# One written order for three engines from the first instruction on: the first batch's attention, its mixing and the weight conversion at fixed places, and k loaded first

## The chip, the cores and the metric

The kernel runs on one core of one Trainium2 chip. The metric is the device time of one execution in microseconds (us). Before the change it is 1892.02 us, the median of 3 runs (1890.05 to 1893.53). Six names come back throughout: PE is the matrix engine (TensorE), DVE the vector engine, ACT the scalar engine, POOL the GpSimd engine, SP the engine whose queue issues almost all DMAs, and PEld is the loading of a matmul's stationary operand, which overlaps PE.

## What is computed

Eight batches of 576 tokens go through three stages, all in fp32: attention with keys and values averaged over groups of 8 tokens, a mixing layer of rank 32 with a feed-forward block behind it, and a Fourier mixing with normalisation and a second feed-forward block.

```python
# attention: q, k, v are (8 batches, 8 heads, 576, 64)
k_p = k.reshape(B, H, 72, 8, D).mean(axis=3)
v_p = v.reshape(B, H, 72, 8, D).mean(axis=3)
scores = scale * np.matmul(q, k_p.transpose(0, 1, 3, 2))
attn = softmax(scores)
x = np.matmul(attn, v_p)              # laid out as (8, 576, 512)
# first block: U (576, 32), V (32, 576), w_ch1 (512, 2048), w_ch2 (2048, 512)
h = x.transpose(0, 2, 1) @ U @ V
u = x + h.transpose(0, 2, 1)
x = u + np.maximum(u @ w_ch1, 0.0) @ w_ch2
# second block, with weights of its own
u = x + np.real(np.fft.fft(np.fft.fft(x, axis=1), axis=2))
un = (u - mean(u)) / np.sqrt(var(u) + 1e-06)
out = u + np.maximum(un @ w_ch1, 0.0) @ w_ch2
```

## The kernel before

**Number format.** A matmul runs on fp32r operands, so each fp32 number is kept as a high part and a low part (`split`: ACT copies the high part, a subtraction on DVE or POOL gives the low part), and one product is three matmuls: high by high, high by low, low by high. The weights arrive as 64-bit floats. For each tile of 128 x 512 weights ACT runs two operations (`high`, L146 and L149) and DVE two integer operations (`bits`, L153 and L154) that build fp32; then comes `split`, on ACT and POOL. `w_first` does this for the 32 tiles W[k, f] of the first block: k = 0 is the first layer, k = 1 the second, f = 0 to 15 a slice of 128 of the 2048 hidden channels.

**Stages.** The work of the first block is cut into groups. A group takes 512 tokens through the feed-forward block: for each f, `st1` makes 12 matmuls of 512 columns into the hidden slice (tile h; its inputs are the transposed tokens utx, called `xs` in the code), ACT and DVE form the high and low part hh and hl, and `st2` of the slice before makes 12 matmuls of 512 columns that add into four output banks (o, o, h, m). One f is called a slot here. Groups 0 to 5 go this way. From about 800 us on, the rest of the first block and all of the second go through a form with 7 products instead of 8 (tiles x, wr).

**What runs beside the groups.** Between the pieces of a slot, generators ("lanes") are stepped: `lane_a` is the attention of batches 1 to 7, one tile of 128 tokens at a time (`kq`: scores and exponentials; `exp_turn`: transposition; `av`: product with v, normalised into x, split into xh and xl; `hu_mm`: the product with U, two matmuls on xh and xl, made right behind the next tile's `kq`), and from batch 3 on the mixing of the batch before (`mix_one`) beside it. `lane_prep` loads and pools k and v. `w_first`, later `w_combine` and `w_second`, convert and combine weights. `pair_prep` reloads the mixed tokens `ud` of the next group from memory, and turns (`turn`, a DVE transpose) and splits them (`settle`) into utx.

**The first batch.** Nothing of group 0 can start before batch 0 has been through attention (`first`, `tile_steps`), the product with U (tile hu, `hu_mm`), the mixing with V (`mix_split`, `mix_mm`; tiles hst, vst) and the transposition (`block_prep`, L826). Three tiles are in flight at a time, on three pairs of PSUM banks (s, o, h). The weight conversion starts in the same stretch.

**What sets the order.** A scheduler of the framework orders each engine's instructions by its own estimate of times, unless `manual_schedule` is on: then the instructions of the engines named stand in the order of the code. Before the change, this holds for PE, ACT and DVE from group 1 on:

```python
    for gi, js in enumerate(groups):
        if gi == 1:
            order.enter_context(tc.manual_schedule(engines={mybir.EngineType.PE, mybir.EngineType.Activation, mybir.EngineType.DVE}))
```

SP and POOL stay with the scheduler in both kernels. Each engine works off its own list strictly in order, and waits on semaphores of the others.

## Time and profile before

| what | value |
|---|---|
| median of 3 runs | 1892.02 us (1890.05 to 1893.53) |
| profiled execution, its own time | 1891.17 us |
| its span, first to last instruction | 1889.1 us |
| PE busy | 1812.9 us, 96% of the span |
| DVE, ACT, POOL busy | 54%, 37%, 10% |
| mean granted clock of PE | 0.984 of full speed |

How to read it: a busy share is the time with an instruction under way. The profiled execution takes 2.07 us more than its span (1891.17 against 1889.1), and lies 0.85 us under the median of the runs. The granted clock is 1.0 at 2.4 GHz and 0.5 at 1.2 GHz; values between are a mean over a stretch that has both. "Idle before" is the time that an engine stood still ahead of an instruction, and the name behind the arrow is what ended it. Matmuls are pipelined, so the times of neighbours overlap.

### The profile page before, as it was taken

How to read it: one execution, taken by the hardware profiler on the slowest of the kernel's cores; microseconds unless marked ns; L12 is line 12 of the kernel's file. 1: busy time of each engine (PE TensorE's matmuls, PEld its weight loads, DVE VectorE, ACT ScalarE, POOL GpSimd, SP SyncE). 2: the span in 40 equal slices, each digit the busy share in tenths (PEclk: the TensorE clock that was granted, in tenths of full speed). 3: DMA queues.
4: the chain of work that ended last, by engine and by line, in shares of the span. 5: the costliest groups of instructions: out<-in, count | busy, mean ns of one | idle time of the engine just before them, and what ended most of it. 6: DMA issues, size and time to landing. Idle time of an engine off the chain costs nothing.

```text
span 1889.1 us, 29426 instructions
## 1 busy us (share of the span) xinstructions
PE 1812.9 (96%) x10424; PEld 1588.1 (84%) x10424; DVE 1029.2 (54%) x2275; ACT 700.1 (37%) x1992; POOL 191.2 (10%) x341
## 2 busy tenths in 40 slices
PE   5898899999999999999999999999999999999999
PEld 4676788788778888899999889989989999999998
DVE  7783667666756444444455655565554444444332
ACT  6662445545544222233333433333323323232321
POOL 4340132122200000000010000000000000000000
PEclk8898999999999999999999999999999999999999
DMA  9652657867857622567678767777777675757564
GB/s 360 243 162 71 186 176 214 260 218 233 247 169 211 194 87 72 186 226 247 223 232 260 268 206 224 226 235 227 218 225 210 201 236 173 238 180 228 184 208 133
DMA packets 264467, 391.90 MB, mean 207 GB/s; under 512 B 61504, under 2 KB 92320, under 8 KB 264320
## 3 DMA queue, kind: packets, MB, share of 16 engines
q1 hardware_dynamic: 263392, 386.61, 64.7%
q0 software_dynamic: 928, 3.40, 0.6%
q8 instruction: 83, 1.36, 0.3%
q14 instruction: 64, 0.52, 0.1%
HBM read 311.55 MB, written 78.38 MB: 206 GB/s over the span
## 4 chain that ended last, share of the span: by engine, by line
PE 83%; DVE 8%; DMA 3%; ACT 3%; issue 2%; SPq 1%; DVEq 0%; ACTq 0%
PE h L114 39%; PE o L114 19%; PE m L114 10%; PE hu L114 7%; PE s L114 7%; PE s L936 1%; DVE scr L154 1%; DMA ul<-ud 1%; DVE x L107 1%; DVE x L577 1%; ACT xh L110 1%; DVE scr L153 1%; PE s L563 1%; DMA raw<-vr 1%; DVE hl L1024 1%
## 5 line engine op out<-in xcount | busy, mean ns | idle before, releaser
L114 PEld LDWEIGHTS h<-x,wr 128*128 128x128 f32 x4032 | 529.1, 191 | 24.3 <-DVE side L107 0.2
L114 PE MATMUL h<-x,wr 128*128 128x256 f32 x4032 | 548.4, 284 | 0.0
L114 PE MATMUL o<-w,hh 128*128 128x512 f32 x1152 | 328.5, 395 | 3.1 <-ACT hh L1023 3.1
L114 PE MATMUL h<-utx,w 128*128 128x512 f32 (+1 forms) x1164 | 285.3, 394 | 16.4 <-ACT utx L110 11.3
L114 PEld LDWEIGHTS h<-utx,w 128*128 128x128 f32 x1164 | 217.6, 191 | 62.3 <-ACT utx L110 11.7
L114 PEld LDWEIGHTS o<-w,hh 128*128 128x128 f32 x1152 | 202.8, 189 | 34.9 <-ACT hh L1023 4.0
L114 PE MATMUL o<-w,hl 128*128 128x512 f32 x576 | 192.3, 392 | 0.0
L107 DVE TENSOR_TENSOR side<-h,side 128x256 f32<-128x256 f32 x192 | 106.3, 554 | 153.5 <-PE h L114 153.0
L114 PE MATMUL m<-w,hh 128*128 128x512 f32 x576 | 166.1, 396 | 0.0
L1319 ACT ACTIVATE hh<-side 128x256 fp32r<-128x256 f32 x192 | 99.9, 521 | 119.7 <-DVE side L107 112.7
L1024 DVE SCALAR_TENSOR_TENSOR hl<-h,hh 128x512 fp32r<-128x512 f32 x96 | 66.2, 690 | 136.4 <-ACT hh L1023 135.9
L1319 ACT ACTIVATE hh<-h 128x256 fp32r<-128x256 f32 x96 | 36.9, 384 | 272.4 <-PE h L114 270.5
L1325 DVE SCALAR_TENSOR_TENSOR hl<-h,hh 128x256 fp32r<-128x256 f32 x96 | 40.7, 424 | 171.3 <-ACT hh L1319 171.3
L114 PEld LDWEIGHTS o<-w,hl 128*128 128x128 f32 x576 | 108.2, 188 | 24.3
L1325 DVE SCALAR_TENSOR_TENSOR hl<-side,hh 128x256 fp32r<-128x256 f32 x192 | 105.9, 551 | 29.4 <-ACT hh L1319 29.4
L114 PEld LDWEIGHTS m<-w,hh 128*128 128x128 f32 x576 | 103.2, 191 | 17.0
L1023 ACT ACTIVATE hh<-h 128x512 fp32r<-128x512 f32 x96 | 57.4, 598 | 145.7 <-PE h L114 140.7
L555 ACT ACTIVATE s<-s,mx 128x72 f32<-128x72 f32 x280 | 83.0, 331 | 61.8 <-DVE mx L551 61.2
L114 PE MATMUL hu<-w,hh 128*128 128x512 f32 x384 | 104.7, 394 | 0.0
L114 PE MATMUL m<-w,hl 128*128 128x512 f32 x288 | 97.9, 394 | 0.0
L104 POOL TENSOR_TENSOR wo<-wo 128x256 fp32r<-128x256 f32 x88 | 66.3, 772 | 261.8 <-ACT wo L110 124.2
L104 DVE TENSOR_TENSOR x<-ul,x 128x256 fp32r<-128x256 f32 x154 | 59.3, 420 | 46.5 <-ACT x L110 46.5
(254 smaller groups left out, 2414.4 us busy)
## 6 DMA issues: line engine op xcount, KB each, us to landing
wr<-wc SPq DMA_DIRECT2D x336, 512.0 KB
wc<-wo SPq DMA_DIRECT2D x88, 256.0 KB
x<-x SPq DMA_DIRECT2D x48, 256.0 KB
ur<-ud SPq DMA_DIRECT2D x36, 256.0 KB
x1d<-ur SPq DMA_DIRECT2D x36, 256.0 KB
ul<-u2d SPq DMA_DIRECT2D x36, 256.0 KB
ur<-u2d SPq DMA_DIRECT2D x36, 256.0 KB
out<-ur SPq DMA_DIRECT2D x36, 256.0 KB
```

The costliest lines, as they stand in the source:

```text
L104: eng.tensor_tensor(out=o, in0=a, in1=b, op=ALU.subtract)
L107: eng.tensor_tensor(out=o, in0=a, in1=b, op=ALU.add)
L110: nc.scalar.activation(out=hi, in_=src, func=ACTF.Copy)
L114: nc.tensor.matmul(o, a, b, start=start, stop=stop, skip_group_check=True)
L153: nc.vector.scalar_tensor_tensor(out=t, in0=hw, scalar=-0x80000000, in1=t, op0=ALU.bitwise_and, op1=ALU.bitwise_or)
L154: nc.vector.scalar_tensor_tensor(out=t, in0=lw, scalar=3, in1=t, op0=ALU.logical_shift_left, op1=ALU.bitwise_or)
L555: nc.scalar.activation(out=s[:, a], in_=v[:, k], func=ACTF.Exp, bias=mx[:, a:a + 1], **kw)
L563: nc.tensor.transpose(e0[:, c * 128:c * 128 + 128], self.s[:, c * 128:c * 128 + 128], ident)
L1023: nc.scalar.activation(out=hh, in_=o, func=ACTF.Relu)
L1024: nc.vector.scalar_tensor_tensor(out=hl, in0=o, scalar=0.0, in1=hh.bitcast(F32), op0=ALU.max, op1=ALU.subtract)
L1319: nc.scalar.activation(out=hh[:, i], in_=c, func=ACTF.Relu)
L1325: nc.vector.scalar_tensor_tensor(out=hl[:, i], in0=c, scalar=0.0, in1=hh[:, i].bitcast(F32), op0=ALU.max, op1=ALU.subtract)
```

## The change

The three engines are put in code order from the start, so every instruction of the first 195 us now stands where the code has it. The code there is written anew: `first` lists the five tiles of batch 0 step by step, with the weight conversion at four written places (`w()`), `mix_first` the mixing and the transposition, and `w_first` does one tile of the conversion in three steps. SP issues k first, then two tiles of q, then v, the other q tiles, and U and V (which went through POOL's queue before). In group 0, one step of each lane stands between the pieces of a slot instead of two or three. In all groups three smaller things change: `xl` is subtracted by POOL instead of DVE, `mix_one` of the tile beside stands ahead of the split in `av`, and `turn` loads both tiles of a block at once. An exponential on a one-column tile at the start loads ACT's table.

```diff
-    mhalf = const.tile([128, 1], F32, name="mhalf")
+    mhalf = const.tile([128, 2], F32, name="mhalf")
+    order = ExitStack()
+    order.enter_context(tc.manual_schedule(engines={mybir.EngineType.PE, mybir.EngineType.Activation, mybir.EngineType.DVE}))
     nc.vector.memset(mhalf, -0.5)
+    nc.scalar.activation(out=mhalf[:, 1:2], in_=mhalf[:, 0:1], func=ACTF.Exp)
...
-    def w_first(tmp):
+    def w_first(at):
...
+        for f in range(5):
+            load(f)
+        for f in range(NF + 1):
+            if f < NF:
+                ts[f] = place(f)
+                high(raws[f][0], 512, ts[f][0], True)
+            if f:
+                bits(raws[f - 1][1], 512, ts[f - 1][1])
+            yield
+            if f < NF:
+                high(raws[f][1], 512, ts[f][1], True)
+                bits(raws[f][0], 512, ts[f][0])
+            yield
+            if f:
                 for k in range(2):
...
+                    w = wp.tile([128, 2, 512], F32R, tag=f"w{k}_{f - 1}", name="w")
+                    W[k, f - 1] = w
+                    split(w[:, 0], w[:, 1], ts[f - 1][k].bitcast(F32), nc.gpsimd)
...
+            yield
...
+        def load_first(self):
...
+            for i in range(4):
+                k(i)
+            self.q_load(0)
+            self.q_load(1)
+            for i in range(5):
+                v(i)
+            for i in range(2, 5):
+                self.q_load(i)
...
+        def first(self, w):
...
+            self.hu_mm(0, 1, self.x0[1], None)
+            w()
+            self.v_high(0)
+            self.v_high(1)
+            self.turn0(3)
+            self.av0(3)
+            self.hu_mm(0, 2, self.x0[2], None)
+            w()
+            self.v_bits(0)
+            self.turn0(4)
+            self.av0(4)
+            self.hu_mm(0, 3, self.x0[3], None)
+            self.hu_mm(0, 4, self.x0[4], None)
+            self.v_bits(1)
+            self.v_split()
+            w()
+            w()
+            self.mix_split(0)
...
         def av(self, b, t, beside):
...
+            if beside:
+                self.mix_one(b - 1, t)
+                if t < 4:
+                    self.mix_load(b - 1, t + 1)
             xh = self.p.tile([128, DM], F32R, tag="xh", name="xh")
             xl = self.p.tile([128, DM], F32R, tag="xl", name="xl")
-            split(xh, xl, xf)
+            split(xh, xl, xf, nc.gpsimd)
...
+        z = [utile_d("ul") for _ in range(NT)]
         for t in range(NT):
...
+            load_blocks(z[t], ud, j * T + t * 128)
+        for _ in range(3):
             yield
...
-            while (1, min(f + 2, NF - 1)) not in W:
+            while (1, min(f + 1, NF - 1)) not in W:
                 step("w")
...
+                if gi == 0:
+                    for name in ("w", "prep", "p"):
+                        step(name)
+                    continue
```

Three places show what moves. The first is DVE's list while tiles 3 and 4 of batch 0 are at work. scr_136 and scr_137 are their normalised outputs before the change, scr_139 and scr_140 after it; lines with wraw are the weight conversion, kp the pooling of batch 1's k, scr_179 the conversion of V. Before:

```order
L413 TENSOR_REDUCE kp<-raw 128x72
L153 SCALAR_TENSOR_TENSOR scr_458<-wraw,scr_458 128x512
L413 TENSOR_REDUCE kp<-raw 128x72
L153 SCALAR_TENSOR_TENSOR scr_458<-wraw,scr_458 128x512
L154 SCALAR_TENSOR_TENSOR scr_458<-wraw,scr_458 128x512 x2
L153 SCALAR_TENSOR_TENSOR scr_482<-wraw,scr_482 128x512 x2
L512 TENSOR_TENSOR scr_136<-s_435,sm 128x512
L154 SCALAR_TENSOR_TENSOR scr_482<-wraw,scr_482 128x512 x2
L512 TENSOR_TENSOR scr_137<-o_464,sm 128x512
L153 SCALAR_TENSOR_TENSOR scr_514<-wraw,scr_514 128x512 x2
```

And after, from the output of tile 3 to the low part of hst:

```order
L543 TENSOR_TENSOR scr_139<-s_403,sm 128x512
L156 SCALAR_TENSOR_TENSOR scr_382<-wraw,scr_382 128x512
L157 SCALAR_TENSOR_TENSOR scr_382<-wraw,scr_382 128x512
L156 SCALAR_TENSOR_TENSOR scr_179<-scr_172,scr_179 128x288
L157 SCALAR_TENSOR_TENSOR scr_179<-scr_172,scr_179 128x288
L536 TENSOR_REDUCE sm<-scr_337 128x8
L537 TENSOR_SCALAR sm<-sm 128x8
L538 RECIPROCAL sm<-sm 128x8
L543 TENSOR_TENSOR scr_140<-o_431,sm 128x512
```

Ahead of the output of tile 4 DVE now has two conversion operations (scr_382) in all; before there were 16, of which this piece shows the last eight.

The second place is PE's list at the end of group 0. hst,vst is the mixing of batch 1 (five matmuls), s<-k,q the scores of batch 2's first tile, h<-utx,w an `st1`, o, h and m with w,hh and w,hl an `st2`. Before, the first `st1` of group 1 (h_1672) stands here behind the mixing:

```order
L114 MATMUL hu<-xl,ust 128x512
L114 MATMUL s_1262<-hst,vst 128x512
L114 MATMUL s_1283<-hst,vst 128x512
L114 MATMUL s_1286<-hst,vst 128x512
L114 MATMUL s_1295<-hst,vst 128x512
L114 MATMUL s_1304<-hst,vst 128x512
L114 MATMUL s_1611<-k,q 128x144 x2
L114 MATMUL s_1612<-k,q 128x144 x2
L563 MATMUL s_1652<-ident,s 128x128 x4
L564 MATMUL s_1653<-ident,s 128x128
L114 MATMUL h_1672<-utx,w 128x512 x12
```

After, the mixing stands in slot 11 of group 0:

```order
L117 MATMUL h_1337<-utx,w 128x512 x12
L117 MATMUL s_1354<-hst,vst 128x512
L117 MATMUL s_1357<-hst,vst 128x512
L117 MATMUL o_639<-w,hh 128x512 x2
L117 MATMUL o_639<-w,hl 128x512
L117 MATMUL o_643<-w,hh 128x512 x2
L117 MATMUL o_643<-w,hl 128x512
L117 MATMUL s_1378<-hst,vst 128x512
L117 MATMUL s_1381<-hst,vst 128x512
```

Four more `st1` with their `st2` follow it there before the first `st1` of group 1.

The third place is DVE's list around one tile of the later batches: s_2532 and s_2710 are the products with v, `x<-s_2544,x` and `x<-s_2718,x` the mixing of the batch before, mx the maxima of the next tile's scores. Before:

```order
L577 TENSOR_TENSOR x<-s_2532,sm 128x512
L104 TENSOR_TENSOR xl<-x,xh 128x512
L107 TENSOR_TENSOR x<-s_2544,x 128x512
L107 TENSOR_TENSOR wo<-w 128x256 x4
L416 TENSOR_REDUCE vp<-raw 128x64
```

After:

```order
L673 TENSOR_TENSOR x<-s_2710,sm 128x512
L110 TENSOR_TENSOR x<-s_2718,x 128x512
L151 TENSOR_SCALAR wo<-cv 128x256
L647 TENSOR_REDUCE mx<-s_2740 128x4
L647 TENSOR_REDUCE mx<-s_2741 128x4
```

The subtraction of xl has left DVE, and the mixing follows the normalisation at once.

## Rows read from the trace of the kernel before

**Rows 1.** The page: busy time of PE, and its granted clock in 40 slices.
```profile
PE 1812.9 (96%) x10424; PEld 1588.1 (84%) x10424; DVE 1029.2 (54%) x2275; ACT 700.1 (37%) x1992; POOL 191.2 (10%) x341
...
PEclk8898999999999999999999999999999999999999
```

**Rows 2.** Four stretches: length, then busy PE, PEld, DVE, ACT, POOL, clock, DMA.
```profile
12.50:47.10 34.60, 26.95 (x125) 21.01 (x125) 33.41 (x64) 29.82 (x86) 15.36 (x17) 0.87 1.05 388
47.10:61.40 14.30, 6.48 (x22) 4.63 (x21) 14.21 (x21) 10.92 (x21) 5.86 (x4) 0.61 1.06 401
61.40:174.00 112.60, 106.94 (x509) 89.39 (x509) 70.35 (x108) 57.98 (x131) 35.43 (x30) 0.97 0.41 130
174.00:195.00 21.00, 6.43 (x19) 3.70 (x19) 10.21 (x18) 6.39 (x23) 0.00 (x0) 0.59 0.64 155
```

**Rows 3.** PE in order of time: start, length, instruction, [idle before, releaser].
```profile
12.52 2.29 PE L114 MATMUL s<-k,scr 128*128 128x144 f32 x8 [12.52 <-ACT k L423]
...
45.06 2.08 PE L114 MATMUL hu<-scr,scr 128*128 128x512 f32 x2 [2.22 <-DVE scr L512]
...
61.41 4.63 PE L114 MATMUL h<-utx,w 128*128 128x256 f32 x24 [3.67 <-DVE utx L104]
...
194.97 4.66 PE L114 MATMUL h<-utx,w 128*128 128x512 f32 x12 [11.31 <-ACT utx L110]
```

**Rows 4.** DVE from 12.5 to 47.1 us by form: count, busy, mean ns, idle before.
```profile
L153 DVE SCALAR_TENSOR_TENSOR scr<-wraw,scr 128x512 int32<-128x512 int32 x9 | 7.8, 871 | 0.7 <-ACT scr L146 0.7
L154 DVE SCALAR_TENSOR_TENSOR scr<-wraw,scr 128x512 int32<-128x512 int32 x8 | 6.8, 871 | 0.0
...
L413 DVE TENSOR_REDUCE kp<-raw 128x72 f32<-128x576 f32 x2 | 1.4, 724 | 0.0
```

**Rows 5.** DVE at the start, in order of time.
```profile
8.03 0.75 DVE L413 TENSOR_REDUCE kp<-scr 128x72 f32<-128x576 f32 x1 [6.53 <-DMA scr<-kT]
9.34 2.20 DVE L413 TENSOR_REDUCE kp<-scr 128x72 f32<-128x576 f32 x3 [0.56 <-DMA scr<-kT]
```

**Rows 6.** The first issues of SP's queue, in order of time.
```profile
0.74 1.01 SPq L444 DMA_DIRECT2D q<-qT  x2
1.79 1.93 SPq L398 DMA_DIRECT2D scr<-kT  x4
```

**Rows 7.** The chain that ended last, 60 to 200 us: start, length, what.
```profile
70.74 2.72 PE h L114 x12
...
132.28 1.37 PE s L114 x10
...
138.67 0.98 PE s L114 x8
...
185.00 2.79 DMA ul<-ud
...
190.43 3.09 DMA ul<-ud
```

**Rows 8.** What PE waited for, 195 to 880 us: total, times, longest.
```profile
PE s L114 <- DVE x L107: 12.6, 16, 1.3
...
PE s L114 <- DVE x L577: 2.1, 3, 1.6
```

**Rows 9.** One tile of batch 3, all engines in order of time.
```profile
267.95 0.69 DVE L577 TENSOR_TENSOR x<-s,sm 128x512 f32<-128x512 f32 x1
...
268.67 0.63 ACT L110 ACTIVATE xh<-x 128x512 fp32r<-128x512 f32 x1 [1.49 <-DVE x L577]
...
269.34 0.69 DVE L104 TENSOR_TENSOR xl<-x,xh 128x512 fp32r<-128x512 f32 x1 [0.70 <-ACT xh L110]
...
269.95 0.68 DVE L107 TENSOR_TENSOR x<-s,x 128x512 f32<-128x512 f32 x1
...
270.69 0.76 PE L114 MATMUL s<-k,q 128*128 128x144 f32 x4 [0.61 <-DVE x L107]
...
271.51 0.39 PE L114 MATMUL hu<-xl,ust 128*128 128x512 f32 x1
```

**Rows 10.** POOL by form: count, busy, mean ns, idle before.
```profile
L104 POOL TENSOR_TENSOR wo<-wo 128x256 fp32r<-128x256 f32 x88 | 66.3, 772 | 261.8 <-ACT wo L110 124.2 <-DVE wo L104 71.7 <-DMA cv<-w1b 21.6
L104 POOL TENSOR_TENSOR w<-scr,w 128x512 fp32r<-128x512 f32 x28 | 41.4, 1494 | 49.0 <-ACT w L110 45.7 <-DMA raw<-kT 2.0 <-PE h L114 1.4
```

More of the change, by code (lines that the diff above doesn't have):

```diff
@@ new lines, in load, with place @@
+        def load(f):
+            raws[f] = [wp.tile([128, 1024], I32, tag=f"w{k}_{f}", name="wraw") for k in range(2)]
+            for k in range(2):
+                nc.sync.dma_start(out=raws[f][k], in_=(w1a, w2a)[k][f].bitcast(I32))
+        def place(f):
+            if f < NF - 3:
+                t = scratch(f % 2)
+                return [t[:, 512 * k:512 * k + 512].bitcast(I32) for k in range(2)]
+            if f == NF - 2:
+                return [at.p.tile([128, DM], F32, tag="xr", name="t", bufs=2).bitcast(I32) for k in range(2)]
+            return [at.cv().bitcast(I32) for k in range(2)]
@@ L329, in w_swap_split @@
         split(w[:, 0], w[:, 1], w[:, 1].bitcast(F32))
+    xs = mp.tile([128, 3, KD, 2, T], F32R, tag="utx", name="utx", bufs=1)
     class Attn:
@@ L401, in load @@
                     nc.sync.dma_start(out=t[:n, 0:512], in_=vr[b, r0:r0 + n, :])
-                self.raw[i] = t
-            ahead = 9 if b == 0 else 2
-            for i in range(ahead):
+            for i in range(2):
                 load(i)
-                if b == 0 and i > 2 and i != 4:
-                    self.q_load(max(0, i - 4))
             yield
@@ L521, in tile_steps @@
-            store(xd[b][t], xf[:TT[t][1]])
-            self.done[t] = (xh, xl)
-            yield
-        def first(self):
-            todo = list(range(5))
-            act = []
-            while todo or act:
-                if todo and len(act) < 3:
-                    t = todo.pop(0)
-                    act.append((t, self.tile_steps(0, t, t % 3)))
-                with urgent():
-                    for t, g in list(act):
-                        if next(g, 1):
-                            act.remove((t, g))
-                            self.hu_mm(0, t, *self.done.pop(t))
-                yield
+                nc.vector.tensor_reduce(out=mx[:, 4 * i:4 * i + 4], in_=sc[i][:, 0:288].rearrange("p (h k) -> p h k", h=4), op=ALU.max, axis=AX.X, negate=True)
@@ new lines, in first @@
+        def first(self, w):
+            for i in range(4):
+                self.pool_k(0, i)
+                if i % 2:
+                    self.kv_k(0, i - 1, i + 1)
+            self.pool_v(0, 0)
+            self.scores0(0)
+            self.exps0(0)
+            self.pool_v(0, 1)
+            self.pool_v(0, 2)
+            self.scores0(1)
+            self.exps0(1)
+            self.pool_v(0, 3)
+            self.pool_v(0, 4)
+            self.kv_v(0)
+            self.scores0(2)
+            self.turn0(0)
+            self.exps0(2)
+            self.av0(0)
+            self.u_high()
+            self.turn0(1)
+            self.scores0(3)
+            self.u_bits()
+            self.av0(1)
+            self.exps0(3)
+            self.hu_mm(0, 0, self.x0[0], None)
+            self.turn0(2)
+            self.scores0(4)
+            self.av0(2)
+            self.exps0(4)
+            self.hu_mm(0, 1, self.x0[1], None)
[16 more added lines that the diff above has]
+            self.mix_split(0)
@@ L1092, in lane_a @@
                 yield
+            if b == 1:
+                for i in range(QAHEAD):
+                    at.q_load(5 + i)
             at.kv_k(b)
@@ L1260 @@
                     until(lambda: state["u"] >= (gi + 2) * TA)
-                if f == NF - 1:
-                    until(lambda: "p" not in lanes, ["p"])
             hs = st1(js, f, gi == f == 0)
+            if f == NF - 1 and not last:
+                until(lambda: "p" not in lanes, ["p"])
             if last and f >= NOP:
@@ L1299 @@
             hq.append((js, f, hs))
+    until(lambda: "p" not in lanes, ["p"])
     if not df:
```

325 lines of the change are left out of this document (140 added, 185 removed).

## The prediction

> **What bounds the kernel now.** I read the page first. PE is busy for 96% of the span, and the row of its granted clock shows 6 to 9 tenths in the first four slices and nines nearly everywhere behind them [rows 1]: if something can be won, it is in the first 190 us, or in the few waits later on. The view by stretches then says what limits each part of that time. From the first scores to the last product with U (12.5 to 47.1) and from there to the first `st1` (47.1 to 61.4), DVE is busy for 33.41 of 34.6 us and 14.21 of 14.3 us, and PE for far less, at a clock of 0.87 and 0.61 [rows 2]. So DVE bounds the beginning. In group 0 (61.4 to 174) PE takes over: 106.94 of 112.6 us. From 174 to 195 nobody is busy: PE 6.43 of 21.0 us, at a clock of 0.59. The rows of PE say why: the first `st1` of group 1 comes at 194.97 after 11.31 us of idling for utx [rows 3], and the chain shows the two reloads of turned tokens, 2.79 and 3.09 us, in series ahead of it [rows 7]. Behind that, the list of PE's waits up to 880 us has one entry of weight: 16 waits, 12.6 us, for the sum that `mix_one` makes on DVE [rows 8].
>
> **Part 1, k first.** The first reduction of k waits 6.53 us for its load, and the others follow at 9.34 [rows 5]; the first scores start at 12.52 [rows 3]. SP issues k at 1.79, behind two tiles of q at 0.74 [rows 6], and U and V go through POOL's queue at the same time. Now k is at the head. The least gain is the issue, 1.79 - 0.74 = 1.05 us; the most is that plus the bytes that go ahead or beside now (0.52 MB of q, 0.75 MB of U and V), at the 388 GB/s of this stretch [rows 2] 3.2 us, together 4.3. I take 3.0: scores at 9.5. The three loads of U and V that SP now issues cost about 0.5 us each [rows 6] ahead of the weights, which are not touched before tile 2 is through; that is hidden behind the tiles' work. The exponential on one column is hidden too, since ACT waits for k at that time.
>
> **Part 2, five tiles without the conversion.** In 34.6 us DVE did 17 conversion operations (7.8 + 6.8 us) and two reductions for batch 1 (1.4 us) [rows 4]. The written order leaves two of the 17 ahead of tile 4's output. At 0.69 us each (a subtraction of the same size beside an idle POOL, [rows 9]) that leaves 33.4 - 16.0 + 1.4 = 18.8 us of DVE work. Unbroken, the last product with U would end 18.8 us after the first scores; as loose as before it would take 34.6. The conversions had filled DVE's waits within a tile (scores on PE, maxima on DVE, exponentials on ACT, transposition on PE, copies on ACT, product on PE, output on DVE), and now these show. I take 24, nearer to the lower end, since three tiles are in flight: the last product with U ends at 33.5 instead of 47.1.
>
> **Part 3, mixing and transposition.** From there to `st1` it is 14.3 us before. Seven of the conversion operations in this stretch go, 4.8 us, so the bounds are 9.5 and 14.3. What is left is a chain in series, and at its end stands the low part of W[0,0] on POOL, 1.49 us [rows 10], without which the third matmul of `st1` waits. I take 13.3: group 0 starts at 46.8 instead of 61.41.
>
> **Part 4, group 0.** PE's work to the first `st1` of group 1: the first `st1` at the low clock 4.63 [rows 3], then 15 `st1` and 15 `st2` of 2.72 [rows 7], 81.6; five attention tiles with scores 0.98 and product with v 1.37 [rows 7], five transpositions at 0.122 (a matmul of the scores is 0.98/8) 0.6, two matmuls with U at 2.72/12 each 0.45, so 3.4 a tile, 17.0; five mixing matmuls 1.1 and the next scores 1.0. The sum is 105.3. Before, the same took 194.97 - 61.41 = 133.6, so 28 us were idling or low clock. The reload of the tokens is the larger part, and the new order takes it off the path: the mixing of batch 1 stands in slot 11, and four slots of 5.4 us cover the reloads of 5.9 us and the transposes. What is late next is the end of the group: the scores of batch 2 wait for ACT's copy of k, which now stands behind the copies of utx; I put 4 us there. The first attention tile costs some waits too, because DVE's sum of the exponentials stands in its list ahead of conversions that the next slot needs. Together I take 10 us of idling, between 2 and the 20.3 that the two stretches had before (112.6 - 106.9 and 21.0 - 6.4, [rows 2]). Group 1 then starts at 46.8 + 105.3 + 10 = 162.1 instead of 194.97: 32.9 us won. The conversion taken out of the beginning comes back in slots 0 to 4: four operations of 0.69 to 0.87, hl 0.69 and two reductions of 0.7 are 4.9 to 5.6 us of DVE for a slot of 5.44 on PE. That just fits, and is the first rival.
>
> **Part 5, groups 1 to 5.** In the tile of [rows 9] the output x is there at 268.64, xh at 269.30, xl at 270.03, and the mixing sum, which stands behind xl on DVE, at 270.63; PE's second half of the scores waits for it, 0.61 us. After the change the sum follows x and is done at about 269.3, ahead of PE: the 12.6 us go. The 2.1 us for x itself stay. In exchange xl comes from POOL: 269.30 + 1.49 = 270.8, and without its wait PE would want it at 271.51 - 0.61 = 270.9. That holds by a hair when POOL is idle, and not when one of its 88 wo subtractions (0.77) is ahead. Tiles of this short distance are 18 of 30, by the order; at 0.35 us each 6 us go back. The bounds are nothing, and 1.5 us (two wo) for each of the 30, 45 us. I take 0.35 since POOL's wo fill only 66 us in 300. Net 6.6 won. The Trainium skill speaks against this edit: "GPSIMD Engine Reference", section 4.1, keeps elementwise work with two inputs on VectorE, as about twice as fast. The trace agrees, 1.49 against 0.69 us; by that rule alone the 30 subtractions would cost 24 us, by the rows it is PE's wait that counts.
>
> Behind group 5 PE's list is the same as before, and nothing is won or lost there.
>
> **The sum.** 1889.1 - 32.9 - 6.6 = 1849.6 us of span. The profiled execution takes 2.07 us more than its span, so 1851.7, and the median of the runs lies 0.85 above the profiled one: 1852.5, rounded to 1853.
>
> **The rivals.** First, the waits come back: source order makes group 0 as loose as before, with DVE a little over PE's pace in the early slots. Then 20.3 instead of 10 us are idle, and the time is 1863; for it speaks the sum of 4.9 to 5.6 us above, against it that a DVE that is late by one slot still meets an `st2` that stands one slot later. Second, the xl on POOL costs more than the mixing gives: at 1 us for each of 18 tiles the 6.6 turn into a loss of 5.4, 1865. Third, the change does not do what it says: the five tiles take the 34.6 us they took, because the path through them and not DVE's work was the limit; then group 0 starts at 57.4 and the time is 1863. DVE's 33.41 busy of 34.6 us speaks against it. Fourth, slower than before: POOL's subtractions stop DVE for their whole length. In group 0 each slot has two of them for the weights, 2 x 1.49 = 3.0 us; if DVE stood still for all of it, a slot would take 4.9 + 3.0 = 7.9 us where I have 5.44, over 16 slots 39 us more, and with the same in the later tiles, 0.8 us for each of 30, 24 more: 1916. It decides from 2.5 us a slot on, which is when the 39.5 us are used up. Against it: POOL was busy for 15.4 of the 34.6 us at the beginning [rows 2], and the conversions were stretched from 0.69 to 0.87 only, 3 us in all. The skill has the rule to it ("SBUF — State Buffer", section "Who interferes with whom"): the port pair of DVE and POOL is locked for a whole instruction. The stretched conversions agree that there is contention, and not that it stops all of DVE's work.
>
> **How the numbers follow.** The forecast, 1838 to 1862, has 0.66; the first rival with 1862 to 1874 0.14; the second 0.07, the third 0.05, the fourth 0.04; better than 1838 0.02, and a gain that shrinks to nothing through several of these 0.02. A measurement of this kernel tells about 0.2%, 4 us, from no change. The range that leaves out less than 2 in 10 is 1838 to 1874: its low end is 5 us less idling in group 0, all of the 12.6 us, and 4 us less in parts 1 to 3; its high end is the first rival with half of the second or third. Faster than 1888 has 0.94, the same 0.02, slower 0.04.
>
> **What would show it.** Right: the first reduction of k before 5.5 us; the last product with U near 33, the first `st1` between 44 and 51; DVE well below full until then; the first `st1` of group 1 near 162, with under 5 us of idling ahead of it and a clock of 1.0; no wait for the mixing sum, and short waits of hu for xl from POOL. Wrong: DVE as full as before up to 47 us; `st1` in slots 0 to 4 waiting for W, or `st2` for hl; POOL behind PE's longest waits.

## The result, and the profile after

The changed kernel takes 1875.58 us (median of 4 runs, 1873.67 to 1876.45), beside 1891.03 for the kernel before on the same chip: a ratio of 0.9917 (0.9900 to 0.9934). It is faster, by 15.5 us where 39 were forecast, and lies just above the range.

The page of the kernel after; PE's busy time and granted clock, in answer to [rows 1]:

```profile
PE 1813.5 (97%) x10424; PEld 1586.4 (85%) x10424; DVE 1020.5 (54%) x2239; ACT 704.2 (38%) x1994; POOL 231.3 (12%) x373
...
PEclk9899999999999999999999999999999999999999
```

The first and the fourth slice look better (8 became 9), no other. The view by stretches, with the same columns as [rows 2], divides the start into the five tiles, the mixing and group 0:

```profile
8.35:36.80 28.45, 22.88 (x125) 18.37 (x125) 20.13 (x46) 16.23 (x58) 3.23 (x9) 1.00 1.06 384
36.80:49.84 13.04, 6.18 (x21) 4.80 (x21) 9.03 (x14) 6.30 (x12) 0.00 (x0) 0.60 1.05 395
...
49.84:182.95 133.11, 115.84 (x522) 93.97 (x523) 93.53 (x142) 82.68 (x178) 56.48 (x47) 0.94 0.53 163
```

DVE is no longer full in the tiles (20.13 of 28.45 us), as forecast. But group 0, from its first `st1` to that of group 1, takes 133.1 us. Before, it was 61.41 to 194.97 [rows 3], 133.6 us. So the 12 us that are won at the start of group 1 (182.95 against 194.97) are those that were won at the start of group 0 (49.84 against 61.41). PE in order of time shows where group 0 stands still:

```profile
8.35 2.26 PE L117 MATMUL s<-k,scr 128*128 128x144 f32 x8 [8.35 <-ACT k L459]
...
35.63 1.12 PE L117 MATMUL hu<-scr,scr 128*128 128x512 f32 x2 [0.43 <-DVE scr L543]
...
49.84 0.80 PE L117 MATMUL h<-utx,w 128*128 128x256 f32 x2 [1.20 <-ACT w L113]
51.20 5.06 PE L117 MATMUL h<-utx,w 128*128 128x256 f32 x22 [0.56 <-POOL w L107]
58.54 4.37 PE L117 MATMUL h<-utx,w 128*128 128x512 f32 x12 [2.28 <-DVE hl L1109]
...
80.47 4.55 PE L117 MATMUL h<-utx,w 128*128 128x512 f32 x12 [3.68 <-DVE hl L1109]
...
165.49 4.61 PE L117 MATMUL h<-utx,w 128*128 128x512 f32 x12 [3.25 <-DVE hl L1109]
...
180.48 1.25 PE L117 MATMUL s<-k,q 128*128 128x144 f32 x8 [2.77 <-ACT k L459]
...
182.95 2.90 PE L117 MATMUL h<-utx,w 128*128 128x512 f32 x12
```

`st1` of a slot writes the one bank h that hl of the slot before has to have read, so it waits for hl. In slots 4 and 14 hl is late, by 3.68 and 3.25 us, and the 12 matmuls behind each of these waits take 4.55 and 4.61 us, not 2.88, at a granted clock of 0.70 and 0.62 in these stretches (columns as above):

```profile
80.47:86.00 5.53, 5.53 (x21) 4.63 (x22) 4.70 (x7) 2.27 (x4) 4.24 (x5) 0.70 0.44 128
...
165.49:170.00 4.51, 4.51 (x13) 3.54 (x14) 3.54 (x6) 1.26 (x2) 1.82 (x3) 0.62 0.99 318
```

Why hl is late stands on DVE:

```profile
75.91 0.67 DVE L431 TENSOR_REDUCE vp<-raw 128x64 f32<-128x512 f32 x1
79.13 0.69 DVE L431 TENSOR_REDUCE vp<-raw 128x64 f32<-128x512 f32 x1 [2.54 <-DMA raw<-vr]
79.74 0.68 DVE L1109 SCALAR_TENSOR_TENSOR hl<-h,hh 128x512 fp32r<-128x512 f32 x1
...
164.08 0.75 DVE L426 TENSOR_REDUCE kp<-raw 128x72 f32<-128x576 f32 x1 [2.74 <-DMA raw<-kT]
164.75 0.68 DVE L1109 SCALAR_TENSOR_TENSOR hl<-h,hh 128x512 fp32r<-128x512 f32 x1
```

The reduction that pools v (or k) of the next batch waits 2.54 (2.74) us for its load, and hl stands behind it. Three reductions stand in a slot of 5.44 us. There are two buffers `raw`, so the load of piece i + 2 can be issued only when piece i is reduced, and then it has SP's queue ahead of it, in order too:

```profile
75.47 0.52 SPq L211 DMA_DIRECT2D wc<-w  x1
76.09 0.56 SPq L443 DMA_DIRECT2D raw<-vr  x1
...
156.62 4.05 SPq L914 DMA_DIRECT2D ul<-ud  x4
160.76 0.57 SPq L440 DMA_DIRECT2D raw<-kT  x1
```

The late load of v stands behind a store of converted weights (wc from w), the late load of k behind reloads of tokens.

Behind group 0, PE's waits from 185 to 870 us (total, times, longest) answer to [rows 8], here of the kernel after:

```profile
PE hu L117 <- POOL xl L107: 7.3, 10, 1.5
```

The 12.6 us of waits for the mixing sum are gone. Instead hu waits for xl from POOL.

### The profile page after: what moved, and what is told of

It is laid out like the page before. It is cut to its first block, busy times and chain, and to the rows that moved or that the text cites. A ratio compares the mean times of both kernels' runs of the same rounds, so it can differ in the third digit from the quotient of the medians.

```text
span 1873.5 us, 29377 instructions
## 1 busy us (share of the span) xinstructions
PE 1813.5 (97%) x10424; PEld 1586.4 (85%) x10424; DVE 1020.5 (54%) x2239; ACT 704.2 (38%) x1994; POOL 231.3 (12%) x373
## 4 chain that ended last, share of the span: by engine, by line
PE 76%; DVE 1%; ACT 1%; DMA 0%; issue 0%; POOL 0%; SPq 0%; DVEq 0%; ACTq 0%; POOLq 0%
PE h L117 35%; PE o L117 18%; PE m L117 9%; PE hu L117 7%; PE s L117 5%; PE s L1021 1%; PE s L659 0%; POOL xl L107 0%; DMA wc<-wo 0%; DVE x L673 0%; ACT hh L1374 0%; ACT k L459 0%; DMA x<-x 0%; DVE hl L1380 0%; ACT hh L1108 0%
## 5 line engine op out<-in xcount | busy, mean ns | idle before, releaser
L117 PE MATMUL h<-utx,w 128*128 128x512 f32 (+1 forms) x1164 | 289.1, 399 | 13.6 <-DVE hl L1109 11.9
L117 PEld LDWEIGHTS h<-utx,w 128*128 128x128 f32 x1164 | 222.0, 194 | 61.8 <-DVE hl L1109 13.9
L1374 ACT ACTIVATE hh<-h 128x256 fp32r<-128x256 f32 x96 | 36.8, 383 | 272.5 <-PE h L117 270.5
```

Source lines behind the costliest of these rows:

```text
L117: nc.tensor.matmul(o, a, b, start=start, stop=stop, skip_group_check=True)
L1374: nc.scalar.activation(out=hh[:, i], in_=c, func=ACTF.Relu)
```

## The experiments

Eighteen kernels ran, each timed beside the kernel before, which had medians of 1891.0 to 1892.6 us. Each expectation stands ahead of its result; its theory and its rival are two forecasts for the same edit. "Group 0" is from its first `st1` to that of group 1; "groups 1 to 5" from there to the start of the last `st1` of group 5 in PE's rows. These two columns come from the one profiled execution of each kernel: kernels whose code in groups 1 to 5 is the same differ there by up to 3 us (567.0 to 570.0 for a3, b4, c3, c4, d3 and d4). Where the intervals of two ratios overlap, as those of d1, d2, e1 and, by a hair, a3 with the changed kernel's, the medians alone don't show which is faster.

| kernel | us | ratio (95%) | group 0 | groups 1 to 5 |
|---|---|---|---|---|
| before | 1891.0 | 1 | 133.6 | 579.7 |
| changed | 1875.6 | 0.9917 (0.9900–0.9934) | 133.1 | 574.8 |
| a1: no load waits | 1866.9 | 0.9866 (0.9851–0.9881) | 126.0 | 575.5 |
| a2: pooling paced | 1868.6 | 0.9870 (0.9849–0.9891) | 129.5 | 572.4 |
| a3: xl on DVE | 1870.6 | 0.9884 (0.9867–0.9901) | 133.9 | 569.0 |
| a4: copy of k first | 1870.6 | 0.9885 (0.9870–0.9900) | 131.6 | 573.2 |
| b1: scheduler until group 1 | 1883.0 | 0.9952 (0.9937–0.9967) | 142.7 | 577.5 |
| b2: old code in order | 1947.2 | 1.0290 (1.0274–1.0306) | 174.0 | 579.4 |
| b3: xl on DVE, sum behind | 1887.4 | 0.9975 (0.9964–0.9985) | 134.0 | 588.4 |
| b4: a2 + a3 + a4 | 1862.0 | 0.9840 (0.9825–0.9854) | 127.0 | 569.9 |
| c1: before, sum ahead | 1875.6 | 0.9909 (0.9895–0.9924) | 133.7 | 563.3 |
| c2: gaps filled | 1876.5 | 0.9916 (0.9902–0.9929) | 134.0 | 575.0 |
| c3: b4, k pooled earlier | 1859.7 | 0.9828 (0.9814–0.9841) | 125.7 | 568.3 |
| c4: c3, gaps filled | 1860.5 | 0.9829 (0.9813–0.9844) | 126.9 | 567.0 |
| d1: conversion earlier | 1872.8 | 0.9898 (0.9881–0.9915) | 132.2 | 574.6 |
| d2: a3, old turn | 1874.0 | 0.9902 (0.9887–0.9917) | 136.3 | 571.9 |
| d3: c3, conversion earlier | 1857.2 | 0.9816 (0.9799–0.9833) | 122.8 | 570.0 |
| d4: d3, gaps filled | 1855.9 | 0.9811 (0.9794–0.9827) | 120.8 | 569.3 |
| e1: stores off SP | 1872.3 | 0.9888 (0.9871–0.9904) | 130.9 | 574.6 |
| e2: d3, stores off SP | 1858.6 | 0.9819 (0.9804–0.9833) | 122.4 | 573.1 |

**a1, the load waits taken away.**

```diff
             def load(i):
+                if b < 3 and i > 1:
+                    self.raw[i] = self.two[i % 2]
+                    return
...
```

> The changed kernel, with seven of the nine loads of k and v left out for batches 1 and 2 each: the reductions read the first two pieces again, so their work on DVE stays and only their wait for a load goes (and 3.8 MB of transfers). Theory: in group 0 hl stands on DVE behind reductions that wait for loads; PE loses 3.68, 3.25 and 0.51 us of idling and about 1.7 us at the low clock behind each of the two long ones, 11 us in all. Then 9 to 11 us go: 1865 to 1867. Rival: DVE's own work (conversion, reductions, sums) is what makes hl late, the load waits only fill its slack. Then nothing goes: 1874 to 1877, and the first matmuls of slots 4 and 14 still wait for hl.

1866.9 us, and group 0 takes 126.0 instead of 133.1. In the list of PE's waits (total, times, longest), the kernel after has in its group 0, from 49.84 to 182.95,

```profile
PE h L117 <- DVE hl L1109: 9.7, 4, 3.7
```

and a1, from 50.93 to 176.96,

```profile
PE s L117 <- ACT k L465: 3.7, 2, 2.8
...
PE h L117 <- DVE hl L1115: 2.3, 1, 2.3
```

Three of the four waits for hl are gone, so the theory holds: the loads' lateness makes hl late, and not DVE's own work, which is still there (93.5 us busy in group 0 of both kernels). Of the 11 us in the list of the theory some 4 came back in group 0: the copy of k is waited for twice now, and the clock that had fallen twice in group 0 falls at its end instead.

**a2, the same with all the loads.** Batch 1's pieces of v are loaded early, into buffers that are free then, and the pooling of batch 2 is paced:

```diff
...
-            while b - 1 not in started or (b == 2 and state["slot"] < 11):
+            while b - 1 not in started or (b == 2 and state["slot"] < 4):
...
                     for name in ("w", "prep", "p"):
-                        step(name)
+                        if name != "prep" or f < 4 or i == 1:
+                            step(name)
```

> The changed kernel, computing everything: batch 1's five pieces of v are loaded at once into buffers that are free at that time, and the pooling of batch 2 stands in slots 4 to 14 with one reduction a slot instead of three a slot from slot 11. Theory of the load waits: as without the loads, 1865 to 1868, with hl on time in slots 4, 14 and 15. Rival (DVE's work): the same number of reductions, now beside attention tiles, so 1875 to 1880, with new waits for hl or for x in slots 6 to 10.

1868.6, just above what was expected. The waits in slots 14 and 15 are gone, and none has come in slots 6 to 10. But in slot 3 of this kernel the third piece of k is late, as DVE shows:

```profile
74.09 0.75 DVE L426 TENSOR_REDUCE kp<-raw 128x72 f32<-128x576 f32 x1 [5.08 <-DMA raw<-kT]
```

It was issued at 63.40, behind six loads of weights (58.8 to 62.4 us in SP's rows). So the theory holds, with one long load wait left.

**a3, xl back on DVE.**

```diff
-            split(xh, xl, xf, nc.gpsimd)
+            split(xh, xl, xf)
```

> The changed kernel with one part undone: xl is subtracted by DVE again, in the same place of the written order, behind the mixing sum. Theory: POOL's subtraction costs the waits of hu for xl that the trace shows, 7.3 us in groups 1 to 5 and about 3 us in group 0, and DVE has room for 35 operations of 0.69 us; so 5 to 10 us go, 1866 to 1871, and hu no longer waits for xl. Rival: what POOL costs PE, DVE would cost it too, in late hl and maxima: 1874 to 1880.

1870.6, in total what the theory had. Groups 1 to 5 gain 5.8 us, and of the 7.3 us of waits for xl this is left:

```profile
PE hu L117 <- DVE xl L107: 1.6, 6, 0.5
```

Group 0, where about 3 us were expected, gains nothing (133.9). The Trainium skill ("GPSIMD Engine Reference", section 4.1) would not have made this edit of the change, since it puts elementwise work with two inputs on VectorE. The run agrees, 1870.6 against 1875.6 us.

**a4, the copy of k first.**

```diff
...
             if f == NF - 1:
+                if gi == 0:
...
+                    at.kv_k(2)
                 if not last:
                     for t in range(NT):
                         settle(groups[gi + 1][1], t)
```

> The changed kernel with the two ACT copies of batch 2's k moved ahead of the copies of utx in slot 15 of group 0. Theory: the 2.77 us that the first scores of batch 2 wait for that copy go, and the low clock does not come into it: 1872 to 1873.5. Rival: the wait goes on to the next thing that is late there (the copies of utx now come two operations later, and the first matmuls of group 1 wait for them): 1875 to 1877.

1870.6, more than expected; the wait of 2.77 us has become 0.16. In this kernel's profile the two waits of slots 14 and 15 had other lengths too (2.29 and 3.03), so a part of the gain beyond 2.8 us is not explained.

**b1 and b2, the written order alone and the new code alone.** b1 turns the manual order on at `gi == 1`, as before the change. b2 is the kernel before with the order of its code from the first instruction.

> The changed kernel's code, but with the scheduler's order on PE, ACT and DVE until group 1, as before the change. Theory: the written order is what shortens the beginning, so without it the 11.6 us that were won up to the first matmul of group 0 go back, at least in part, and group 0 comes out differently by a few us either way: 1882 to 1890. Rival: k first, the shorter code of the conversion and the mixing in slot 11 make the gain, and the order itself nothing: 1872 to 1878, with group 0 at 48 to 51 us.

> The kernel before, not otherwise changed, with PE, ACT and DVE in the order of its code from the first instruction on. Theory: its code was not written to be an order; five tiles and the conversion then stand on DVE as they come, waits for loads and all, so it is slower than before, 1895 to 1925. Rival: source order is a gain of itself, 1878 to 1886.

b1 takes 1883.0 us, but not for the reason given. The start of group 0 is hardly lost: it comes at 48.22, with a wait of 3.38 us inside the first `st1`, so that slot 1 begins at 60.36 instead of 58.54. So of the 11.6 us the new code of the beginning (k first, other places of the conversion) wins nearly 10 under the scheduler too. What the order is worth lies at the end of group 0, where PE of b1 waits for the turned tokens:

```profile
190.87 5.79 PE L116 MATMUL h<-utx,w 128*128 128x512 f32 x12 [13.82 <-ACT utx L112]
```

b2 takes 1947.2. Its PE waits in order behind engines that wait in order:

```profile
112.70 2.29 PE L116 MATMUL s<-k,q 128*128 128x144 f32 x8 [21.74 <-ACT k L425]
```

**b3 and c1, the order of a tile.** b3 undoes both edits of `av` in the changed kernel. c1 makes one of them in the kernel before, where `mix_one` had stood behind `av`:

```diff
...
+            if beside:
+                self.mix_one(b - 1, t)
+                if t < 4:
+                    self.mix_load(b - 1, t + 1)
             xh = self.p.tile([128, DM], F32R, tag="xh", name="xh")
...
```

> The changed kernel with both of its changes to the later tiles undone: xl on DVE, and the mixing sum behind it. Theory: these two together are worth the 5.0 us that groups 1 to 5 have become shorter (579.7 to 574.8 us), xl on DVE alone 5.8 us more; so this kernel loses 10 to 11 us to the one with only xl on DVE (1870.6), 1880 to 1882, with PE waiting some 12 us for the mixing sum again. Rival: the other edits of the change (both tiles loaded at once, conversion one slot ahead) made groups 1 to 5 shorter; then it stays at 1871 to 1876.

> The kernel before, with one part of the change alone: in the later tiles the mixing sum stands ahead of the split of x; xl stays on DVE. Theory: the 12.6 us that PE waits for that sum go, and xl, which comes one sum later, costs 1 to 2 us of waits of hu, as in the changed kernel with xl on DVE (1.6 us): 1880 to 1883. Rival: the sum ahead is worth this only together with the rest of the change (with that rest, and without the sum ahead, groups 1 to 5 took 588.4 us, 8.7 more than before): then less than 4 us go, 1888 or more.

Both went further than the theory. c1, one part of the change alone, takes 1875.6 us, as much as the whole change; its groups 1 to 5 are 16.4 us shorter, PE waits for no mixing sum, and for no xl at all. b3 loses 19.4 us to a3 in groups 1 to 5, and ends 8.7 behind the kernel before there; by the medians it loses 16.7, and its 12 runs spread over 8.7 us (1882.6 to 1891.3). So the sum ahead of the split is worth more than the waits in [rows 8] (12.6 us): in the stretch of groups 1 to 5 PE idled 18.1 us before and 6.0 in c1, and its busy time fell by 4.4 us, from 564.5 to 560.2 us. The two rows, of the kernel before and of c1, run to the end of that last `st1`:

```profile
194.97:777.58 582.61, 564.52 (x2751) 472.04 (x2752) 345.11 (x746) 240.38 (x850) 84.95 (x139) 0.99 0.60 185
```
```profile
196.78:762.96 566.18, 560.15 (x2751) 471.69 (x2752) 345.09 (x746) 240.62 (x850) 85.22 (x139) 0.99 0.62 191
```

Why the busy time fell is not shown. And something else in the change costs groups 1 to 5 about 5.7 us, which d2 looks for.

**b4 and c3, the mended kernel.** b4 puts a2, a3 and a4 together and pools the late pieces of k last. c3 loads the third piece early too, into the buffer of the transposed exponentials (tile e), and pools k in the middle; of its edit this is the order of the pooling, against the changed kernel:

```diff
...
-            for i in range(9):
+            for i in (0, 1, 4, 5, 2, 6, 3, 7, 8) if b == 1 else range(9):
...
```

> The changed kernel with what the first runs showed put together: batch 1's v loaded early into free buffers and the two late pieces of its k pooled last, batch 2 pooled with one reduction a slot from slot 4, xl on DVE, k's copies ahead of those of utx. Theory: the terms add up: group 0 takes 129.5 us with the paced pooling, less the 5.1 us wait and 1.5 us of low clock that were left in slot 3, less 2.7 for the copy of k, 120 to 121 us; groups 1 to 5 take 569 as with xl on DVE; so 1856 to 1860. Rival: they don't add up, since a wait that goes uncovers the next (DVE has more to do in slots 4 to 10 with xl and the reductions): 1863 to 1867.

> The mended kernel (1862.0) with one more edit: the third piece of batch 1's k is loaded early too, into the buffer of the transposed exponentials, and k is pooled in the middle, not last. Theory: the first scores of batch 1 waited 3.59 us for ACT's copy of k because the last two pieces of k were pooled last; that wait and the low clock behind it (about 2 us) go: 1856 to 1859. Rival: in slots 2 to 4 DVE, POOL and ACT are behind with the conversion, and k comes no earlier: 1861 to 1864.

b4 takes 1862.0, between theory and rival: groups 1 to 5 are as expected (569.9), group 0 is 127.0 and not 120 to 121. c3 takes 1859.7, between the two again. Its first scores of batch 1 still wait 2.58 us for the copy of k, though the last reduction of that k on DVE starts at 75.17 us. ACT shows what its copy, at 81.44, stands behind:

```profile
78.90 0.68 ACT L149 ACTIVATE scr<-wraw 128x512 int32<-128x512 uint32 x1 [3.53 <-POOL w L107]
...
81.44 0.88 ACT L469 ACTIVATE k<-kp 64x288 f32<-64x288 f32 x2
```

The copy stands behind a conversion that waits for POOL, and POOL, in c3, for the pooled v:

```profile
75.42 0.51 POOL L475 TENSOR_TENSOR v<-vp,vmask 128x192 f32<-128x192 f32 x1 [3.37 <-DVE vp L431]
75.89 2.98 POOL L107 TENSOR_TENSOR w<-scr,w 128x512 fp32r<-128x512 f32 x2
```

It is the same fault once more, on other engines: lists in order, and the wait of one item of the background goes through all of them to PE.

**c2 and c4, PE's gaps filled.** Matmuls without a reader keep PE busy ahead of group 0:

```diff
+            o = bank("h0")
+            for _ in range(6):
+                mm(o, ident, self.x0[0], True, True)
             self.v_split()
...
```

> The changed kernel with 14 more matmuls, whose results nobody reads, in PE's three gaps ahead of group 0 (six in the wait for the low part of hst, five and three in the waits for the transposition and for utx). Theory: slots 0 and 1 run at the low clock because PE did little in the 13 us before (6.2 us busy); with the gaps filled the first st1 takes 3 to 3.5 instead of 5.9 us and slot 1 about 5.5 instead of 7.2 to 8.1; less about 1 us by which the added matmuls may hold up the products: 3 to 5 us go, 1870 to 1873. Rival: the clock is set by something else, or slot 1 waits for hl(0) anyway: nothing goes, 1875 to 1877.

> The kernel with k pooled early and the gaps of PE filled, both. Theory: the gains add, 1852 to 1856. Rival: a faster slot 0 and 1 only brings PE sooner to conversions that are not ready (W of slots 2 and 3): the same as with k early alone, within 2 us.

Neither gains (1876.5 and 1860.5). PE of c2 shows why; the clock from 36.8 to 50 us is 1.00 now, not 0.60:

```profile
36.80:50.00 13.20, 10.91 (x43) 6.11 (x41) 9.71 (x16) 6.71 (x12) 0.66 (x1) 1.00 1.05 394
```
```profile
50.66 2.90 PE L117 MATMUL h<-utx,w 128*128 128x256 f32 x22 [0.85 <-POOL w L107]
57.98 5.49 PE L117 MATMUL h<-utx,w 128*128 128x512 f32 x12 [4.41 <-DVE hl L1117]
```

The first `st1` takes 2.90 us instead of 5.06, and the wait behind it grows from 2.28 to 4.41. hl(0) comes when ACT has been through the conversion of the next weights (its row at 52.34 in c2 waits 2.56 us for POOL), so the low clock of slot 0 costs nothing.

**d1, d3 and d4, the conversion earlier.** Two steps more of it are done within the tiles, where DVE and POOL had room, a third one moves up, and the split of hst (`mix_split`) goes ahead of the last two:

```diff
             self.hu_mm(0, 0, self.x0[0], None)
+            w()
             self.turn0(2)
...
+            w()
             self.hu_mm(0, 1, self.x0[1], None)
-            w()
...
             self.turn0(4)
+            w()
             self.av0(4)
...
             self.v_split()
+            self.mix_split(0)
             w()
             w()
-            self.mix_split(0)
```

> The changed kernel with two steps of the weight conversion more inside the five tiles, so that it is two thirds of a slot further on when group 0 begins, and with the split of hst ahead of two conversion operations. Theory: the first slots are bound by the chain of the conversion through ACT, DVE and POOL (POOL's subtractions of the weights begin 5.8 to 6.3 us apart there, a slot on PE is 5.44), and hh(0) stands behind it on ACT; then the start of group 0 comes 1 to 2 us earlier, the wait of 2.3 us in slot 1 shrinks, and 2 to 5 us go: 1870.5 to 1873.5. Rival: only the load waits count in group 0, and the conversion is hidden: 1874.5 to 1877; or it gets in the way of the tiles, whose last product with U then ends 1 to 2 us later: 1876 to 1878.

> The mended kernel with k pooled early (1859.7), and the conversion two steps further on. Theory: its waits of 2.58 us for the copy of k and 2.66 us for e come from ACT, which stands in order behind the conversion and so behind POOL; a conversion that is ahead takes them away, at least the first: 1853 to 1857. Rival: POOL's rate bounds the conversion, and its lead is gone by slot 3: 1858 to 1861.

> As the one before, with PE's gaps ahead of group 0 filled with 14 matmuls whose results nobody reads. With the conversion behind, the faster clock gave nothing, since hl(0) was late. Theory: with the conversion ahead, hl(0) comes with the end of st1(0), and the 2.2 us that st1(0) gains at full clock are kept: 2 to 4 us less than without. Rival: as before, no difference beyond 1 us.

The median of d1 is 2.8 us below the changed kernel's, as its theory had it, and that of d3 2.5 below c3's, at the edge of its own; each of these pairs has overlapping intervals. The rows agree with d1's theory: group 0 of d1 starts at 47.18, and slot 1 waits 1.41 us for hl and not 2.28. But d3 still waits 2.58 us for the copy of k and 2.64 for e (the transposed exponentials), as c3 did, so that half of its theory fell: a conversion that is two steps ahead does not get past POOL's list. d4 is 1.3 us better than d3, too little to be told from nothing with the intervals in the table. d3 has the lowest median without idle matmuls, and is faster than the changed kernel and than the kernel before: 0.9816 (0.9799 to 0.9833).

**d2, the old turn.** a3 with the tiles of a block reloaded and transposed one after the other, as before the change.

> The changed kernel with xl on DVE and the turn of a block one tile after the other, as before the change. With xl on DVE groups 1 to 5 took 569.0 us, with the sum ahead in the kernel before 563.3. Theory: the two transposes of a block behind each other on DVE make hl and xl late; with them apart groups 1 to 5 take 563 to 565 us; the boundary of group 0, which has less time for the reloads, may lose what is won. Rival: the turn has nothing to do with it (tiles stand at other places of the slots): 568 to 570 us.

The theory is wrong: groups 1 to 5 take 571.9 us, not 563 to 565. That is above the rival's 568 to 570 too, because PE waits once for the turned tokens, which it does not in a3 (PE's waits from 195 to 870 us):

```profile
PE h L117 <- ACT utx L113: 3.5, 1, 3.5
```

Group 0 takes 2.4 us more than in a3. So loading both tiles at once is not what costs the 5.7 us. The wait speaks for a gain by it, but the medians, 3.4 us apart with overlapping intervals, don't settle that.

**e1 and e2, the stores off SP's queue.** Nothing but the issuer of 24 stores changes; on ACT they stand in code order, behind group 0:

```diff
         def plain(w, n):
-            nc.sync.dma_start(out=wc[0][n].rearrange("p (h x) -> p h x", h=2), in_=w)
+            nc.scalar.dma_start(out=wc[0][n].rearrange("p (h x) -> p h x", h=2), in_=w)
```

> The changed kernel with the 24 stores of plain weights (wc from w) issued by ACT, at their place in the code behind group 0, and not by SP, where the scheduler puts them between the loads of k and v. SP's rows show it standing for 7.8 us between 60 and 85 us at such stores, whose weights POOL has not made yet; the load that DVE waits 2.54 us for was issued at 76.09, behind a store at 75.47, though its buffer was free at about 73.7. Theory: SP's queue, and not the number of buffers, makes that load late; then the first st1 that waits for hl in slot 4 comes 2 to 4 us earlier, and 2 to 5 us go in all, 1870.5 to 1873.5; the stall of slot 14, behind the reloads of tokens, stays. Rival: with two buffers the loads are late anyway: 1875 to 1877.

> The mended kernel with the conversion earlier (1857.2) and the same stores issued by ACT. Its loads of k and v are not waited for any more, so by either theory it is the same within 2 us, 1855.5 to 1859, unless the issues on ACT cost something there.

e1 takes 1872.3 us, as the theory had it, and e2 is the same as d3 within 1.4 us. The medians of e1 and the changed kernel are 3.3 us apart with intervals that just overlap; the rows decide. In e1 PE's rows show slot 4 nearly without its wait, and slot 14 with it:

```profile
79.36 3.06 PE L117 MATMUL h<-utx,w 128*128 128x512 f32 x12 [0.24 <-DVE hl L1109]
...
163.96 4.60 PE L117 MATMUL h<-utx,w 128*128 128x512 f32 x12 [2.83 <-DVE hl L1109]
```

So with two buffers the loads can come in time in slot 4. What made the one late was SP, which between 60 and 85 us of the kernel after waits for POOL's weights:

```profile
SPq L211 <- POOL w L107: 7.8, 4, 4.6
```

## Why the prediction was wrong

The span is 1873.5 us where the sum had 1849.6. Of these 23.9 us group 0 makes 17.8, parts 1 to 3 make 3.0, groups 1 to 5 make 1.6 and the rest of the kernel 1.4.

**Parts 1 and 3** held. The first reduction of k came at 3.65 us, the scores at 8.35 (4.2 us won, 3.0 forecast). Mixing and transposition took 13.1 us (13.3 forecast).

**Part 2** was too short: from the first scores to the last product with U it took 28.4 us, where I had 24. I took DVE's work (18.8) as the lower bound, and left out PE's, which stood in [rows 2]: 26.95 us at a clock of 0.87, so 23.4 at full clock. After the change PE is busy for 22.88 of the 28.45 us, and its waits are the rest: 2.8 us for ACT's copies of the transposed exponentials, 1.3 for a load of q, 0.7 for POOL, 0.6 for DVE. Together parts 1 to 3 gave 11.6 instead of 14.6 us. That they come from the written order was wrong as well: with the scheduler back, b1 keeps nearly 10 of them.

**Part 4** is the step that failed: "Group 1 then starts at 46.8 + 105.3 + 10 = 162.1". Group 0 took 133.1 us, not 115.3. Of the 17.8 us too much, 7.3 are idling (133.1 - 115.8 = 17.3 us, where I took 10). The idling comes neither from the work on DVE that the first rival feared (DVE was busy for 93.5 of 133.1 us) nor mainly from the end of the group: the 2.77 us for the copy of k were foreseen as 4. I counted the pooling as two reductions of 0.7 us a slot. It was three, and the price was not their work but their waits for loads. I had costed DVE's list and not SP's, though the scheduler still orders SP's, and the loads stand there behind stores that wait for POOL. In the kernel before, PE waited for no hl in group 0; source order puts the waiting reduction ahead of it. a1, a2 and e1 show this cause and its size, 7.1, 3.6 and 2.2 us of group 0. The other 10.5 us are PE's own time, and the 105.3 us that I took for it were too few from the start: before the change PE was busy for 106.94 + 6.43 = 113.4 us of this stretch [rows 2], with 528 matmuls against 522 after it. I let all of that excess go but the first `st1` at the low clock. By the rows, the low clock in `st1` of slots 0, 1, 4 and 14 makes 5.86 - 4.63 = 1.2, 4.37 - 2.88 = 1.5 and twice 1.7, 6.1 us in all, which my sum did not have, because it had no stalls that long; the part in slot 0 would only have become waiting (c2). An attention tile takes some 3.8 us and not 3.4 (from `st1` at 89.09 to that at 143.37 it is 54.3 us; less six slots of 5.44 and 3.8 us of listed waits, 17.8 are left for five tiles without the first scores and the first transposition, which stand ahead of 89.09 and take 0.9 and 0.5), 2.2 us for five. Some 2.2 us I did not take apart.

But these 18 us are not all to be had by mending the pooling. d3, without load waits, still takes 122.8 us: waits for the copy of k (2.7), for e (2.9), for hl (1.4) and for xh (1.0) are left. The first two stand on ACT behind a conversion that waits for POOL (3.54 us at 72.72, 1.63 at 107.38). The other two don't: ahead of that hl ACT waits for PE's first `st1` itself, and ahead of that xh for DVE's normalised output.

**Part 5** came out near its sum, 5.0 us of 6.6, by luck: its two terms were both larger, and the change costs these groups something that I had no term for. The terms are waits of hu for xl of 7.3 us, 10 times (6 forecast, 18 times), and a3 prices the edit at 5.8 us; the sum ahead of the split is worth 16.4 us in c1, where I had only its waits, 12.6. What is left over remains open: groups 1 to 5 take 569.0 us in a3 and 563.3 in c1, with the same order within a tile. It is not the turn (d2). Idling makes 4.0 of it (10.0 against 6.0 us), spread over many short waits, for hl, for xl, for the copies of k. Whether the tiles' other places within the slots cause it was not tried.

**Behind group 5** the order is the same, and the time from the last `st1` to the end went from 1114.4 to 1115.8 us. The other kernels lie between 1112.7 and 1116.8, so this is scatter.

**The rivals.** The first, "the waits come back", had the right place and nearly the right idling (20.3; measured 17.3), with the wrong reason, and 1862 to 1874 for the time ended just below 1875.6. The second named a cost that is there (5.8 us in a3), but the mixing sum gives more: groups 1 to 5 became 5.0 us shorter, not longer. The third is wrong: the tiles took 28.4, not 34.6 us. The fourth is wrong in size: DVE operations beside POOL's were stretched in some places (below), and the kernel was faster. The high end of the range, 1874, was summed wrong as well: the first rival's 1863 with half of the second or of the third gives 1868 to 1869, and 1874 takes half of both. And the row of the clock in [rows 1] has 8 and 9 tenths in its first four slices, not 6 to 9; no number hangs on that.

## What to carry to other kernels

When engines are taken from a scheduler's order to a written one, look in each list, the DMA queue's too, for what may wait (a load, another engine's background work) and at what stands behind it. Count the waits there, not the durations: here reductions of 0.7 us ahead of hl cost PE 7 us of group 0. Load background data early and use one piece a slot, and keep stores that wait off the queue that loads, as long as something waits for these loads (e1 gained by it, e2 did not). Make the small edit alone as well: the sum ahead of the split gave in the old kernel all that the whole change gave.

## What the runs showed of the hardware

DVE's integer operation on two operands in SBUF, 0.69 us by itself, can take more than twice as long beside a subtraction on POOL. In the kernel after, on DVE and on POOL:

```profile
73.61 0.68 DVE L156 SCALAR_TENSOR_TENSOR scr<-wraw,scr 128x512 int32<-128x512 int32 x1
74.40 1.59 DVE L157 SCALAR_TENSOR_TENSOR scr<-wraw,scr 128x512 int32<-128x512 int32 x1
```
```profile
73.67 1.77 POOL L107 TENSOR_TENSOR w<-scr,w 128x512 fp32r<-128x512 f32 x1 [3.28 <-ACT w L113]
```

The Trainium skill ("SBUF — State Buffer", section "Who interferes with whom") says that a DVE instruction with two inputs in SBUF contends with a GpSimd instruction that reads SBUF. The second row on DVE agrees; the first lies beside the same subtraction from 73.67 on, and took 0.68 all the same. Of the 64 such operations in the trace (L156 and L157, 128x512), the 40 with no two-input operation of POOL beside them took 0.64 to 0.70 us; of the 24 others 13 took more than 0.75, at most 1.75.

The low clock behind a wait is not fixed by the wait's length: after 2.29 us of idling in slot 14 the twelve matmuls of a4 took 3.02 us, after 2.22 us in the same slot of c2 4.28 us. And PE at the low clock can cost nothing, where the next thing it needs is late anyway (c2).
